# One expert in three items of 256 rows with lists known step by step, the other seven in items of 768 rows

## The chip, the cores and the metric

The kernel runs on one core of a Trainium2 chip. The core has five engines that run their own instructions in order: TensorE (PE; its weight loads are PEld), VectorE (DVE), ScalarE (ACT), GpSimd (POOL) and SyncE (SP); SyncE issues most DMAs, GpSimd those that gather and scatter rows by an index. The metric is the device time of one execution in microseconds, the median of several runs. A profile is one execution with its own time; its rows are shown further down.

## What is computed

A gated linear attention over 4 sequences of 768 steps and 8 heads of 48, whose output is the input of a mixture of 8 experts with 2 chosen for each of the 3072 tokens (32-bit floats throughout):

```python
f = 1.0 / (1.0 + np.exp(-f_logit))
for t in range(S):
    state = f[:, :, t, :, None] * state + np.einsum('bhd,bhe->bhde', k[:, :, t], v[:, :, t])
    y[:, :, t] = np.einsum('bhd,bhde->bhe', q[:, :, t], state)
x = y.transpose(0, 2, 1, 3).reshape(B * S, H * D)           # 3072 x 384
noisy = x @ w_gate + np.log1p(np.exp(x @ w_noise)) * noise  # 8 experts
# top2: the two largest of each token; top2_w: softmax of the two
for e in range(E):
    for k in range(2):
        mask = top2[:, k] == e
        h = np.maximum(x[mask] @ w1[e], 0.0)                # 384 -> 1024
        out[mask] += top2_w[mask, k, None] * (h @ w2[e])    # 1024 -> 384
```

## The kernel before

**Attention.** The sequence is cut into 6 chunks of 128 steps, and with 4 sequences that makes 24 rounds. A round has seven stages: `forget` (transposes f, exponential and logarithm on ScalarE), `summed` (a running sum on VectorE), `decays` (exponentials on ScalarE), `scaled` (transposes q and k, products on VectorE), `scores`, `output` and `features` (three blocks of matmuls). The loop over `i` (L1551) starts the stages of several rounds, each with its own lag, in an order written out by hand, and every engine's instructions stay in the order in which the loop issues them (`in_order`). Loads go into rings of 5 (f), 4 (q, k) and 6 (v) tiles by SyncE; `clamp` limits the f tile from below, on VectorE for the first two tiles, on GpSimd for the others. The first loads stand ahead of the loop. `warm_up` issues matmuls of ones while TensorE has nothing else, four in each of the three rounds before round 0. `load_router` brings the router's weights by eight small DMAs of GpSimd's queue.

**Router.** After a chunk's four rounds `route` finds the two experts of its 512 tokens and each token's place in its expert's list. Eight puts a chunk (`put`, L705, indirect DMAs of GpSimd) write the entries (row, gate, token) into `lists` in DRAM; the rows themselves lie in `x_rows`. A list grows chunk by chunk in order, so its first entries are final before the last chunk is routed. `first_loads` fetches and gathers the first lists within the attention's loop; what the kernel takes for granted about list lengths it checks with flags (`enough`, `plan`), and a raised flag starts the general path (`general`) behind the main one.

**Items.** The experts' work is cut into items, each a list of pairs (expert, first entry) of 256 rows; `p` counts pairs and `k` items. Three kinds exist before: items 0 and 1 are the first 256 rows of experts 0 and 1, taken from the lists of three chunks (`NE` = 2); items 2 and 3 are the other 512 rows of experts 1 and 0; items 4 to 9 are the 768 rows of experts 2 to 7 (`WIDE`). What a list has beyond 768 entries goes through five small remainder blocks (`quarter_block`), spread over five of the 768-row items.

- A 256-row item: `first_layer` (L955), four pieces of six matmuls `hp` and an activation by ScalarE, then `second_layer` (L1223), seven products of four matmuls (a Strassen form), each a piece. The product order is 1, 7, 4, 5, 6, 2, 3; their operands come from `second_sums` over w2 (VectorE, into `u`) and `inner_sums` over the hidden rows. The results of products are copied and scaled on ScalarE (`P17`, then the gates) and added on VectorE into `ys`, and two scatters (`scatter`, indirect DMAs that add) put them into `out`: one behind the fifth product, one behind the seventh.
- A 512-row item: `first_of_two` (L972), 44 matmuls of 256 columns with sums of weights and rows by VectorE (`first_sums`).
- A 768-row item: `first_of_three` (L1088), 15 products for each of four blocks of w1, in an order written out by hand (`ORDER`); sums of weights (`SUMS_W`) and of rows (`SUMS_T`) by VectorE are made during the item before. `late_second_layer` then runs three times, once for each 256 rows.

**Rows on their way to an item.** `fetch` reads 256 list entries (SyncE), `gather` brings their rows in two halves of 128 (GpSimd) into `xg`, a ring of four pairs. Rows must then be transposed. `turned` does it on TensorE (three transposes a half) with a copy out of PSUM. For 768-row items ScalarE parts the rows' 16-bit halves (`split`), SyncE issues a transposing DMA (`flip`), and ScalarE puts the halves together (`joined`). These steps stand between the products of the item before (`between`, in `second_parts`). A matmul over 256 columns needs both halves.

**Order around the change.** Behind the attention's loop the pieces of the items are issued one by one (L1643). Around each piece the loop issues zeros for `out` (SyncE, 192 KB each), fetches up to six pairs ahead, gathers by a rule on the item and the piece, one or two steps of the router, and all puts that are ready. Scatters of different items wait for each other, since they add to the same `out`. `weights` and `part_of_weights` load w1 and w2 into two places each, `home` says which item uses which; w2 of expert 1 is loaded in four parts between the attention and the loop over the items.

## Time and profile before

| | us |
|---|---|
| median of 3 runs | 623.33 |
| lowest and highest | 622.68, 626.96 |
| the profiled execution's own time | 622.47 |
| its span, first to last instruction | 620.7 |
| matmuls busy on TensorE | 605.5 |
| weight loads busy on TensorE | 555.6 |
| VectorE busy | 455.6 |
| ScalarE busy | 363.8 |
| GpSimd busy | 277.7 |

The span is that of the trace; the execution's time also has what lies around it. Busy times of engines overlap. The mean granted clock of TensorE over the span is 0.993 of full speed. Line numbers (L961) are those of the kernel before. A releaser is the last of what an instruction waited for, as far as the profile's semaphore events show it.

### The profile page before, as it was taken

The page shows a single profiled execution, that of the slowest core. Times are in us where ns is not written, and L with a number is a line of the kernel's source. Part 1 is how long each engine was busy: PE and PEld are TensorE (multiplying, and loading weights), DVE is VectorE, ACT ScalarE, POOL GpSimd, SP SyncE. Part 2 cuts the span into 40 slices and gives each one's busy share as a digit, 9 for nine tenths or more (in the row PEclk, how much of TensorE's full clock was granted, in tenths as well). Part 3 has the DMA queues.
Part 4 walks back from the last instruction along what each step waited for, and adds up shares of the span by engine and source line. Part 5 has one row for each costly group of instructions (what it writes and reads, how often), then busy time and mean ns, then how long its engine had stood idle before and what let it go on. Part 6 is the DMA issues. An engine that isn't in the chain of part 4 may idle for free.

```text
span 620.7 us, 13321 instructions
## 1 busy us (share of the span) xinstructions
PE 605.5 (98%) x4846; PEld 555.6 (90%) x4846; DVE 455.6 (73%) x1051; ACT 363.8 (59%) x890; POOL 277.7 (45%) x305
## 2 busy tenths in 40 slices
PE   8999999998999999999999999999999999999995
PEld 7999998887898889998899899899988998998995
DVE  6777868697575575888787887787877877877840
ACT  6877676753223343477756766676577467646611
POOL 6824688768774614052163316323440624241032
PEclk9999999999999999999999999999999999999998
DMA  9999988886907547368398559848873894361024
GB/s 182 191 231 200 194 170 171 187 182 195 282 8 231 128 134 168 129 108 256 128 216 179 154 154 204 242 105 218 136 254 118 204 209 129 71 145 23 0 26 56
DMA packets 183082, 98.00 MB, mean 158 GB/s; under 512 B 147600, under 2 KB 176272, under 8 KB 183008
## 3 DMA queue, kind: packets, MB, share of 16 engines
q1 hardware_dynamic: 170832, 77.81, 48.6%
q0 software_dynamic: 12176, 19.25, 17.3%
q8 instruction: 40, 0.66, 0.4%
q14 instruction: 34, 0.28, 0.2%
HBM read 69.68 MB, written 19.62 MB: 144 GB/s over the span
## 4 chain that ended last, share of the span: by engine, by line
PE 89%; DMA 4%; POOL 2%; DVE 1%; issue 1%; SPq 1%; ACT 0%; POOLq 0%; DVEq 0%; ACTq 0%
PE y L1293 30%; PE E L1123 7%; PE D L1123 7%; PE C L1123 5%; PE B L1123 5%; PE xp L628 4%; PE sc L575 4%; PE y L593 4%; PE hp L961 2%; PE y L604 2%; PE P L986 2%; PE kp L535 2%; PE A L1123 2%; PE fp L535 2%; PE ds L599 1%; PE qp L535 1%
## 5 line engine op out<-in xcount | busy, mean ns | idle before, releaser
L1170 POOL DMA_INDIRECT out_dram<-ys,slots x48 | 88.0, 1833 | 225.8 <-DVE ys L1299 156.4
L1293 PE MATMUL y<-qk_all,f_all 128*128 128x192 f32 x528 | 93.5, 326 | 1.0 <-ACT ys L1309 1.0
L1293 PEld LDWEIGHTS y<-qk_all,f_all 128*128 128x128 f32 x528 | 86.8, 190 | 1.6 <-ACT ys L1309 1.5
L1299 DVE SCALAR_TENSOR_TENSOR ys<-y,slots,ys 128x192 f32<-128x192 f32 x66 | 27.4, 416 | 55.6 <-PE y L1293 17.6
L855 POOL DMA_INDIRECT xg<-x_rows,slots x48 | 50.7, 1056 | 35.9 <-issue 23.5
L1293 PE MATMUL y<-w,hs_b 128*128 128x192 f32 x352 | 64.4, 326 | 0.0
L1293 PEld LDWEIGHTS y<-w,hs_b 128*128 128x128 f32 x352 | 58.6, 190 | 0.4
L707 POOL DMA_INDIRECT lists<-entry,sloti x48 | 51.2, 1066 | 10.5 <-issue 7.6
L1131 ACT ACTIVATE hs_b<-hs_b 128x256 f32<-128x256 f32 x120 | 50.2, 418 | 5.8 <-DVE hs_b L1135 4.4
L1342 ACT ACTIVATE ys<-y,slots 128x192 f32<-128x192 f32 x22 | 9.2, 420 | 58.5 <-PE y L1293 52.1
L608 ACT COPY yT<-y 128x256 f32<-128x256 f32 x48 | 15.7, 376 | 36.3 <-PE y L604 24.3
L578 DVE TENSOR_TENSOR A<-sc,causal 128x1024 f32<-128x1024 f32 x24 | 29.3, 1222 | 8.8 <-PE sc L575 8.6
L1293 PE MATMUL y<-qk_all,hs_b 128*128 128x192 f32 x176 | 32.9, 330 | 0.0
L1293 PE MATMUL y<-w,f_all 128*128 128x192 f32 x176 | 32.7, 329 | 0.0
L1293 PEld LDWEIGHTS y<-qk_all,hs_b 128*128 128x128 f32 x176 | 28.8, 190 | 2.4 <-issue 2.1
L900 ACT COPY planes<-xg 128x768 uint16<-128x768 uint16 x36 | 29.3, 826 | 2.5 <-DMA xg<-x_rows,slots 2.5
L549 DVE TENSOR_TENSOR_SCAN L<-f,cap 128x512 f32<-128x512 f32 x24 | 29.6, 1232 | 0.5 <-ACT cap L544 0.5
L1158 DVE TENSOR_TENSOR f_all<-hs_b 128x512 f32<-128x512 f32 x44 | 29.9, 683 | 0.0
L1293 PEld LDWEIGHTS y<-w,f_all 128*128 128x128 f32 x176 | 28.9, 190 | 0.7
L1009 ACT ACTIVATE hs_b<-hs_b 128x256 f32<-128x256 f32 x32 | 12.9, 417 | 27.0 <-DVE hs_b L1006 20.3
L1128 ACT COPY hs_a<-D 128x256 f32<-128x256 f32 x66 | 24.4, 370 | 7.2 <-PE D L1123 5.4
L529 POOL TENSOR_SCALAR f_all<-f_all 128x384 f32<-128x384 f32 x22 | 26.2, 1193 | 4.1 <-DMA f_all<-in_f_logit_dram 4.1
(282 smaller groups left out, 1583.7 us busy)
## 6 DMA issues: line engine op xcount, KB each, us to landing
w<-in_moe_w_dram SPq DMA_DIRECT2D x12, 1536.0 KB
w_q<-in_moe_w_dram SPq DMA_DIRECT2D x10, 1536.0 KB
w<-in_moe_w_dram SPq DMA_DIRECT2D x16, 384.0 KB
f_all<-in_f_logit_dram SPq DMA_DIRECT2D x24, 192.0 KB
...
```

The source lines that it names most:

```text
L535: nc.tensor.transpose(p[:, cols(hp)], flat[:, cols(hp)], ident)
L549: nc.vector.tensor_tensor_scan(L[n], data0=logf[n], data1=cap[n % 2].rearrange("d a t -> d (a t)"), initial=0.0, op0=ALU.add, op1=ALU.min)
L578: nc.vector.tensor_tensor(A[n].rearrange("j r (a i) -> j (r a) i", i=C), sc.rearrange("j r (a i) -> j (r a) i", i=C), causal.unsqueeze(1). ...
L707: into = nc.gpsimd.indirect_dma_start(out=lists, out_offset=bass.IndirectOffsetOnAxis(ap=sloti[:, r, b:b + 1], axis=0), in_=entry[:, c, b, ...
L855: nc.gpsimd.indirect_dma_start(out=xg[p][:, s, :], out_offset=None, in_=x_rows[0:HALF * B * C] if p < NE else x_rows, in_offset=bass.Indir ...
L900: nc.scalar.copy(planes[p][:, s], by_halves(p)[:, s * 2 * DM:(s + 1) * 2 * DM].rearrange("t (d h) -> t h d", h=2))
L1123: nc.tensor.matmul(banks[name, j], lhsT=half_of(x, k)[:, j * 128:(j + 1) * 128], rhs=half_of(y, k), start=first, stop=True, skip_group_che ...
L1131: nc.scalar.activation(at(to, j), at(y, j), AF.Relu, scale=-1.0 if more[0][0] == "-" else 1.0)
L1158: nc.vector.tensor_tensor(sm[which], x, y, op)
L1170: into = nc.gpsimd.indirect_dma_start(out=out, out_offset=bass.IndirectOffsetOnAxis(ap=slots[p][:, s, 2:3], axis=0), in_=ys[s], in_offset= ...
L1293: nc.tensor.matmul(to, lhsT=x[:, o, :], rhs=y[:, o, :], start=(start and o == 0), stop=(o == FH - 1), skip_group_check=not start)
L1299: nc.vector.scalar_tensor_tensor(to, in0=bank, scalar=gate[s], in1=to, op0=ALU.mult, op1=ALU.add)
```

## The change

`NE` becomes 3, and the items are: 0, 1 and 2 with rows 0 to 255, 256 to 511 and 512 to 767 of expert 0, then items 3 to 9 with 768 rows of experts 1 to 7. Items of 512 rows no longer exist, with `first_of_two`, `first_sums` and their helpers. Item 0 takes its rows from the lists of three chunks, as before; item 1 from those of five chunks; item 2 from the full lists (`known`). Item 1's list is fetched behind the 40th put, the last of chunk 4, and gathered behind the 42nd; in the attention's loop only item 0's list is left. A second check, `nearly_enough`, asks for 512 entries after five chunks. The groups that tell the scheduler which DMAs touch different rows (puts, zeros, scatters) follow.

Items 0 to 2 share the first places of w1 and w2, and the `u` sums of item 0 serve all three. Item 1's rows are turned between item 0's last two products, item 2's in item 1's second layer. The sums for item 3, the first of 768 rows, are made in items 1 and 2: `SUMS_W` in both, `SUMS_T` in item 2. Item 3's first pair is turned on TensorE in item 2's first layer, the other two are split and flipped there (behind its second and third step) and joined in its second layer. w2 of expert 1 is loaded in item 2's first four pieces. Remainder blocks start with item 4, as before.

At the start the first loads are in another order: the fourth and fifth f tile stand behind the second q and k tile, the first v tile in the loop. VectorE clamps the third f tile, the router's weights are loaded ahead of the loop, round 0 issues its `scores` ahead of `scaled` and `forget`, and the last of the three groups of four warm-up matmuls goes.

The diff, cut to its core (removed bodies of `first_of_two` and `first_sums` left out):

```diff
-    NE = 2
-    WIDE = 6
-    late_experts = (*range(NE - 1, NE - 3, -1), *range(NE, NE + WIDE), *range(NE - 3, -1, -1))
-    items = [(e, [(e, 0)]) for e in range(NE)]
-    items += [(e, [(e, 256 * i) for i in range(0 if e >= NE else 1, 3)]) for e in late_experts]
+    NE = 3
+    items = [(0, [(0, 256 * i)]) for i in range(NE)] + [(e, [(e, 256 * i) for i in range(3)]) for e in range(1, E)]
     pairs = [p for _, ps in items for p in ps]
     first_of = [sum(len(ps) for _, ps in items[:k]) for k in range(len(items) + 1)]
-    assert NE + WIDE == E and len(pairs) == NP
+    assert len(pairs) == NP
...
+            if c == NCH - 1:
+                tc.declare_no_dep(into.ins, group="nearly full", reason="slots differ")
...
-        lack = rt.tile([1, NE], F32, tag="lack", name="lack", bufs=1)
-        nc.vector.tensor_scalar(lack, total[0:1, 0:NE], 255.5, None, ALU.is_lt)
-        nc.vector.tensor_reduce(short, lack, axis=AX.X, op=ALU.max)
+        nc.vector.tensor_scalar(short, total[0:1, 0:1], 255.5, None, ALU.is_lt)
+        yield
+
+    def nearly_enough():
+        total = one_bank("total_c")[:, 0:E]
+        nc.tensor.matmul(total, lhsT=ones, rhs=upto[NCH - 2][:, :, B], start=True, stop=True)
+        yield
+        nc.vector.scalar_tensor_tensor(short, in0=total[0:1, 0:1], scalar=511.5, in1=short, op0=ALU.is_lt, op1=ALU.max)
         yield
...
     def home(k):
-        return k % NR if k < NE else (NE - 1 + k - NE) % NR
+        return 0 if k < NE else (k - NE + 1) % NR
+
+    def known(p):
+        return (HALF, NCH - 1, NCH)[min(p, 2)]
...
-        if p < NE:
+        if p == 0:
 
             tc.declare_no_dep(got.ins, group="later", reason="slots differ")
             tc.add_to_no_dep_group("full", got.ins)
+        elif p == 1:
+            tc.add_to_no_dep_group("nearly full", got.ins)
 
...
-            nc.gpsimd.indirect_dma_start(out=xg[p][:, s, :], out_offset=None, in_=x_rows[0:HALF * B * C] if p < NE else x_rows,
+            nc.gpsimd.indirect_dma_start(out=xg[p][:, s, :], out_offset=None, in_=x_rows[0:known(p) * B * C],
                                          in_offset=bass.IndirectOffsetOnAxis(ap=slots[p][:, s, 0:1], axis=0))
-            if p < NE:
+            if p == 0:
                 nc.gpsimd.memset(empty[:, 0:LR // 256], 0)
...
-        if NE <= k < NE + NR:
+        if k <= NE:
             return
...
+    def rows_of(k):
+        return wide[0] if k == 2 else xt_a[:, :, k * 256:(k + 1) * 256]
+
...
         k = item_of(p)
         if k < NE:
-            to = xt_a[:, :, k % 2 * 256 + s * 128:k % 2 * 256 + (s + 1) * 128]
+            to = rows_of(k)[:, :, s * 128:(s + 1) * 128]
...
-        (nc.vector.tensor_copy if p < NE else nc.scalar.copy)(to, xp[:, 0:DM].rearrange("d (k t) -> d k t", k=KO))
+        (nc.scalar.copy if p else nc.vector.tensor_copy)(to, xp[:, 0:DM].rearrange("d (k t) -> d k t", k=KO))
...
-            planes[p] = late[-1].tile([128, 2, 2, DM], U16, tag="planes", name=f"planes{p}", bufs=1)
+            if NE < p < NE + 3:
+                planes[p] = wide[1][:, p - NE].bitcast(U16).rearrange("t (s h d) -> t s h d", s=2, h=2)
+            else:
+                planes[p] = late[-1].tile([128, 2, 2, DM], U16, tag="planes", name=f"planes{p}", bufs=1)
...
-            most = min(NP if len(n_put) == NCH * B * 2 else NE, NP if what == "fetch" else done["fetch"])
+            most = min(NP if len(n_put) == NCH * B * 2 else 1, NP if what == "fetch" else done["fetch"])
...
-        if k == NE:
+        if 0 < k < NE:
             return
...
-    def first_sums(k, which):
...
-                    nc.tensor.matmul(hp[:, o, :], lhsT=w1[home(k)][:, i, (fo + o) * 128:(fo + o + 1) * 128], rhs=xt_a[:, i, k % 2 * 256:(k % 2 + 1) * 256],
+                    nc.tensor.matmul(hp[:, o, :], lhsT=w1[home(k)][:, i, (fo + o) * 128:(fo + o + 1) * 128], rhs=rows_of(k)[:, i, :],
...
+            if k:
+                sum_of_three(NE, SUMS_W[fo // 2 if k == 1 else 7 + fo // 2])
+            if k == 2:
+                if fo in (2, 4):
+                    turned(NE, fo // 4)
+                    split(NE + fo // 2, 0)
+                    split(NE + fo // 2, 1)
+                    flip(NE + fo // 2)
+                elif fo == 6:
+                    for t in SUMS_T:
+                        if t[0] == "0":
+                            sum_of_three(NE, t[2:])
             yield
...
-    def first_of_two(k):
...
-            if p < NE:
-                tc.declare_no_dep(into.ins, group="second half", reason="rows differ")
-                tc.add_to_no_dep_group("first half", into.ins)
+            if p < 2:
+                tc.declare_no_dep(into.ins, group=("second half", "last rows")[p], reason="rows differ")
+                tc.add_to_no_dep_group(("first half", "all but last")[p], into.ins)
...
+        if 0 < k + 1 < NE:
+            turns_now = {5: [(k + 1, 0)], 6: [(k + 1, 1)]} if k == 0 else {4: [(k + 1, 0)], 5: [(k + 1, 1)]}
+            if k == 1:
+                sums_now = {i + 1: [SUMS_W[4 + i]] for i in range(3)}
+        elif k + 1 == NE:
+            turns_now = {1: [(NE + 1, 0)], 2: [(NE + 1, 1)], 3: [(NE + 2, 0)], 4: [(NE + 2, 1)]}
+            split_now = {5: NE + 3}
+            sums_now = {3: [t[2:] for t in SUMS_T if t[0] == "1"], 4: [t[2:] for t in SUMS_T if t[0] == "2"]}
...
+        elif is_wide(k + 1):
+            turns_now = {2 + s: [(first_of[k + 1] + q, s)] for s in range(2)}
...
+            if not last:
+                split_now[1] = first_of[k + 1] + q + 1
+            elif is_wide(k + 2):
+                split_now[1] = first_of[k + 2]
...
-    for nm, n in (("f", 0), ("f", 1), ("q", 0), ("k", 0), ("f", 2), ("f", 3), ("q", 1), ("k", 1), ("v", 0)):
+    for nm, n in (("f", 0), ("f", 1), ("q", 0), ("k", 0), ("f", 2), ("q", 1), ("k", 1), ("f", 3), ("f", 4)):
...
-    clamp(2)
-    clamp(3)
...
+    for part in range(2):
+        load_router(part)
+    clamp(3)
...
-            m = (*(m for m in range(NS) if m % NCH < HALF), *(m for m in range(NS) if m % NCH >= HALF))[len(zeroed)]
+            m = [m for cs in (range(HALF), range(HALF, NCH - 1), (NCH - 1,)) for m in range(NS) if m % NCH in cs][len(zeroed)]
...
-        for what, p, pause in (("fetch", 1, 4), ("first", 0, 0), ("second", 0, 3), ("fetch", 2, 5), ("first", 1, 1), ("second", 1, 6),
-                               ("turned", 0, 0), ("fetch", 3, 1)):
+        for what, p, pause in (("fetch", 1, 4), ("first", 0, 0), ("second", 0, 15), ("turned", 0, 0)):
...
+        if i == 0:
+            order[0:3] = order[2], order[1], order[0]
...
-                load("f", n + 4)
+                for m in () if n < 2 else (n + 3,) if n < 5 else (n + 3, n + 4) if n == 5 else (n + 4,):
+                    load("f", m)
...
-                if n in (1, 2):
-                    load_router(n - 1)
+                if n < 2:
+                    load("v", n)
...
-                for m in (n + 1,) if n < 4 else (2 * n - 3, 2 * n - 2) if n < 6 else (n + 3,):
+                for m in () if n == 0 else (n + 1,) if n < 4 else (2 * n - 3, 2 * n - 2) if n < 6 else (n + 3,):
...
+            elif stage is summed and n == 0:
+                clamp(2, nc.vector)
...
-        if i < 0:
+        if i < -1:
...
-                router = chain(router, plan(), beyond())
+                router = chain(router, nearly_enough(), plan(), beyond())
...
-    for part in range(4):
-        part_of_weights(1, 2, part)
...
-        if item < NE or not is_wide(item + 2):
-            return 0
-        return 2 if item == NE else 1 if piece >= 12 else 0
...
+        if item == 2 and piece < 4:
+            part_of_weights(1, 2, piece)
...
-        n = item - NE - 2
+        n = item - NE - 1
...
+            if len(n_put) == (NCH - 1) * B * 2:
+                fetch(1)
+                done["fetch"] = 2
+            elif len(n_put) == (NCH - 1) * B * 2 + 2:
+                gather(1)
+                done["gather"] = 2
```

## Rows read from the trace of the kernel before

**Rows 1.** The page's busy time, share of the span and instructions of each engine.

```profile
PE 605.5 (98%) x4846; PEld 555.6 (90%) x4846; DVE 455.6 (73%) x1051; ACT 363.8 (59%) x890; POOL 277.7 (45%) x305
```

**Rows 2.** TensorE's stretches: the view by windows. Columns: from and to in us, length, busy us and instructions of TensorE's matmuls (PE), its weight loads (PEld), VectorE (DVE), ScalarE (ACT) and GpSimd (POOL), granted TensorE clock as a share of 2.4 GHz, busy share of the DMA engines, GB/s.

```profile
150.00:154.30 4.30, 2.40 (x31) 2.02 (x31) 1.75 (x7) 1.32 (x4) 3.97 (x6) 1.00 0.86 231
154.30:158.70 4.40, 4.39 (x13) 3.54 (x14) 0.95 (x2) 0.48 (x1) 3.91 (x6) 0.61 1.05 385
...
177.80:200.00 22.20, 21.39 (x120) 19.35 (x120) 12.98 (x32) 6.18 (x13) 12.37 (x14) 1.00 0.57 162
200.00:239.70 39.70, 38.73 (x213) 36.05 (x213) 24.98 (x57) 15.18 (x35) 15.99 (x13) 1.00 0.50 112
...
560.00:613.30 53.30, 53.20 (x288) 49.79 (x287) 32.46 (x71) 25.50 (x73) 10.99 (x7) 1.00 0.16 20
613.30:620.70 7.40, 0.00 (x0) 0.00 (x0) 0.00 (x0) 0.36 (x1) 1.55 (x1) 0.63 0.46 62
```

**Rows 3.** Who TensorE waited for: instruction and its line, what released it, us in total, times, longest.

```profile
PE hp L961 <- DVE xt_a L890: 1.9, 1, 1.9
...
PE y L1293 <- ACT ys L1309: 1.0, 1, 1.0
...
PE xgp L889 <- DMA xg<-x_rows,slots: 0.8, 1, 0.8
PE kp L535 <- DMA qk_all<-in_k_dram: 0.5, 1, 0.5
```

**Rows 4.** TensorE's instructions in order of time, those of one line merged: start, length, line, output and inputs, count (each matmul of two 32-bit operands is recorded twice, a transpose once). `hp` and `y` are a 256-row item's two layers, `xgp` the transposes of gathered rows, `E` the first product of a 768-row item.

```profile
167.35 1.46 PE L1237 MATMUL y<-w,hs_a 128*128 128x192 f32 x8
...
173.55 0.49 PE L889 MATMUL xgp<-ident,xg 128*128 128x128 f32 x3
173.88 1.47 PE L1237 MATMUL y<-qk_all,f_all 128*128 128x192 f32 x8
...
176.48 1.46 PE L1237 MATMUL y<-w,f_all 128*128 128x192 f32 x8
177.78 10.52 PE L961 MATMUL hp<-xt_a,w 128*128 128x256 f32 x48
...
277.16 0.59 PE L1123 MATMUL E<-xt_b,w 128*128 128x256 f32 x2
...
303.10 1.46 PE L1293 MATMUL y<-w,hs_b 128*128 128x192 f32 x8
```

**Rows 5.** The chain that ended last, in order of time: start, length, what it waited for. The first two are the third forget load and the third key load; the last three the landing of the last put, the fetch of the full lists and the landing of their first gather.

```profile
3.62 3.45 DMA f_all<-in_f_logit_dram
...
11.41 3.57 DMA qk_all<-in_k_dram
...
181.61 2.89 DMA lists<-entry,sloti
...
184.52 0.37 SPq L844
...
187.39 5.90 DMA xg<-x_rows,slots
```

**Rows 6.** ScalarE's instructions in order of time, with the idle time before them and its releaser.

```profile
15.53 0.63 ACT L554 ACTIVATE P<-L 128x512 f32<-128x512 f32 x1 [1.55 <-DVE L L549]
...
272.48 1.96 ACT L1373 COPY xt_b<-xg 128x768 uint16<-128x768 uint16 x2
...
325.34 0.83 ACT L900 COPY planes<-xg 128x768 uint16<-128x768 uint16 x1 [0.45 <-DMA xg<-x_rows,slots]
```

**Rows 7.** GpSimd's instructions in order of time. L707 is a put into the lists, L855 a gather, L1170 a scatter of an item's output, L1415 that of a small remainder block; from 160 to 206 us, and from 320 and 440 us.

```profile
166.76 1.04 POOL L707 DMA_INDIRECT lists<-entry,sloti  x1 [0.17 <-issue]
...
172.01 0.96 POOL L707 DMA_INDIRECT lists<-entry,sloti  x1 [0.17 <-issue]
...
192.72 1.65 POOL L1170 DMA_INDIRECT out_dram<-ys,slots  x1 [0.30 <-issue]
194.67 1.59 POOL L1170 DMA_INDIRECT out_dram<-ys,slots  x1 [0.30 <-issue]
202.08 1.55 POOL L1170 DMA_INDIRECT out_dram<-ys,slots  x1 [5.82 <-DMA out_dram<-ys,slots]
...
205.79 1.01 POOL L855 DMA_INDIRECT xg<-x_rows,slots  x1 [0.30 <-DMA out_dram<-ys,slots]
...
321.60 1.01 POOL L855 DMA_INDIRECT xg<-x_rows,slots  x1 [1.75 <-DMA slots<-lists]
...
445.58 1.56 POOL L1170 DMA_INDIRECT out_dram<-ys,slots  x1 [4.00 <-DVE qk_all L1086]
451.06 1.34 POOL L1415 DMA_INDIRECT out_dram<-ys_q,slots_q  x1 [3.91 <-DMA out_dram<-ys,slots]
```

**Rows 8.** ScalarE's groups by line: count, busy us and mean ns, idle time before them. L900 is `split`, L1373 `joined`, L963 the activation of a 256-row item's first layer.

```profile
L900 ACT COPY planes<-xg 128x768 uint16<-128x768 uint16 x36 | 29.3, 826 | 2.5 <-DMA xg<-x_rows,slots 2.5
L1373 ACT COPY xt_a<-xg 128x768 uint16<-128x768 uint16 x24 | 25.2, 1054 | 0.0
...
L963 ACT ACTIVATE hs_a<-hp 128x512 f32<-128x512 f32 x8 | 4.8, 597 | 16.9 <-PE hp L961 16.9
```

**Rows 9.** SyncE's queue in order of time: the issue of one `flip`.

```profile
266.78 1.45 SPq L903 DMA_TRANSPOSE xg<-planes  x1
```

**Rows 10.** VectorE's groups by line: one of the `second_sums`.

```profile
L933 DVE TENSOR_TENSOR qk_all<-w 128x768 f32<-128x768 f32 x18 | 17.0, 950 | 0.0
```

143 lines of the change are left out of this document (14 added, 129 removed).

## The prediction

> **What bounds the kernel now.** I read the page's busy times first: TensorE has work for 605.5 of 620.7 us, VectorE for 73% and ScalarE for 59% [rows 1]. So time is won only where TensorE's instructions are removed or where it waits, and lost only where a new wait ends on it. The second view is TensorE by stretches: of the last 768-row item's 53.30 us 53.20 are busy, the closing 7.4 us hold no matmul and stay as they are [rows 2]. The third is what TensorE waited for: 1.9, 1.0, 0.8 and 0.5 us are the waits that matter here [rows 3]. The wait of 1.9 us falls into 150 to 154.3, where TensorE was busy 2.40 of 4.30 us; behind it the granted clock is 0.61 for 4.4 us, that is mostly the lower of the two levels (1.2 and 2.4 GHz) [rows 2]. Those 4.4 us hold one piece of six matmuls, 2.6 us at the price below: 1.8 us lost to the clock. This stretch is not touched by the change (item 0 is fetched, gathered and turned at the same steps of the loop), so I leave it in. The profiled run lasted 622.47 us for a span of 620.7, 1.8 us outside; the median of the three runs is 623.33, 0.9 above the profiled run.
>
> **What is removed on TensorE.** 44 matmuls of a 512-row item are two such items' 88, and 24 a 256-row item's. Before: 2 x 24 + 2 x 44 + 6 x 60 = 496; after: 3 x 24 + 7 x 60 = 492. Sixty take 303.10 - 277.16 = 25.9 us, 0.432 each [rows 4]: 1.7 us less. Transposes of gathered rows: before six lists of 256 x 2 halves x 3 = 36, after four lists = 24; three take 173.88 - 173.55 = 0.33 us [rows 4], so 12 less are 1.3 us. The second layer is 28 matmuls for each 256 rows in either kernel.
>
> By stretches it comes to more, since waits go too. From the start of item 1's first layer (177.78) to the first product of the first 768-row item (277.16) are 99.4 us [rows 4]. After the change the same start leads, one 768-row item further, over: two 256-row items of 24 x 0.432 + 7 x 1.30 (177.78 - 176.48) + 2 x 0.33 = 20.2, with 0.1 of the small count 20.3, and one 768-row item of 25.9 + 21 x 1.30 = 53.2. That is 93.8, 5.6 less, and 5.4 with the added total of five chunks (0.14 as the other such total). In it are the 3.0 of instructions, the 0.8 us wait of the transposes for rows of the full lists and the 1.0 us at the end of the first 512-row item [rows 3]; the other 0.8 is slower starts behind them. **Gain 5.4 if nothing new waits.**
>
> **Start-up.** The third key load was the 13th of SyncE's queue and landed at 14.98 (11.41 + 3.57), the third forget load, the 5th, at 7.07 [rows 5]: 1.0 us a load. TensorE waited 0.5 us for that key load [rows 3]. It is now 11th, 2.0 earlier. Scores of round 0 no longer stand behind two other stages, and four warm-up matmuls go. But at 15.53 ScalarE had waited for VectorE's third scan [rows 6], and VectorE now gets the masking of the first scores ahead of the two products before that scan: what the later start of the mask saved there is spent, and that chain moves by little, 0 to 0.5. On GpSimd's queue the eight router loads now stand ahead of the clamp of the fourth forget load, which TensorE wants a stage later than before. Bounds: 1.5 gained (TensorE's own order) and 0.5 lost (a wait in the thinned warm-up). I take 0.7, nearer the chain.
>
> **Item 1 now needs five chunks' lists.** The last put of chunk 4 starts at 166.76; a put lands 2.9 after its start (181.61 to 184.50), and the first gather starts 2.9 after the fetch (184.52 to 187.39) [rows 5, 7]: 172.5. On GpSimd the gather stands behind the second put of chunk 5 (172.01, 1.6 each) and so starts at 173.6. A gather that started at 321.60 let ScalarE go on at 325.34 [rows 6, 7]: 3.7 us. So the first half is there at 177.3. TensorE comes to its transposes at 167.35 + six products + the small matmuls = 175.8 [rows 4]: it waits 1.5. Then 0.33, a product, 0.33, and the copy to SBUF has no cover before the first layer: 0.8. Item 1 starts 2.3 later than it could.
>
> **Item 2 and the full lists.** The two gathers stand ahead of six puts on GpSimd. Six puts of 1.6 from 176.1 put the last at 184.0 (before: 181.61), and the full lists are fetched 2.4 us later, first gather 189.8 (before: 187.39) [rows 5, 7]. GpSimd now issues six gathers (before: four) ahead of item 0's two scatters: 1.33 each (187.39 to 192.72 for four) to 197.8; second scatter 199.7. Item 1's scatters wait for it to land: 7.4 us from start to next start with zeros on the DMA engines (194.67 to 202.08), 5.5 without (445.58 to 451.06) [rows 7]. They start at 205.2 to 207.1 and take 3.7 (202.08 to 205.79), so the gather of the list of rows 512 to 767 of expert 1 starts at 208.9 to 210.8. I take 209.8.
>
> That gather decides, since item 2's third step of the first layer puts two ScalarE copies of 0.83 (`split`) on those rows, ahead of the activation of its fourth step. Halves land at 213.6 and 214.9, copies end 215.7, activation 0.60 [rows 8]: 216.3. TensorE wants that activation for the third product of the second layer. Without waits it is there at 177.9 + 20.3 + 11.1 (first layer of item 2 with two transposes) + 2 x 1.30 = 212.0, so it is 4.3 late; item 1's 2.3 is inside this, not added to it. Queued behind the blocked copies on ScalarE are the copies of P17, the gate products and four `joined` copies; SyncE's transpose of these rows and two parts of w2 of expert 1 wait too, which VectorE wants only at the end of the first piece of item 3.
>
> **Start of item 3.** Its first product needs both `joined` copies of that list. The last stands on ScalarE behind the scaling of the output, which follows the fifth product: from that product's end three VectorE steps, 0.6 + 0.4 of ScalarE and 1.05 [rows 8] make 3.2, and two products cover 2.6. The transpose itself took at most 5.7 (266.78 on SyncE to the copy at 272.48) [rows 6, 9], which can add 0.6. Behind come two more `split` copies, 1.7, before ScalarE frees the bank that the fourth product wants: 0.7 more. Bounds: 0.6 to 3; I take 1.9.
>
> **Sum.** 620.7 - 5.4 - 0.7 + 4.3 + 1.9 = 620.8. The same 0.1 on the median: **623.4 us, no change.** Costed at nothing: w2 of expert 1 in item 2 instead of before it (its cover is item 2's own 20 us), and the sums for the first 768-row item. They are 24 on VectorE in items 1 and 2; the second sums, four an item of 0.95 [rows 10], drop out there, since all three items share expert 0's weights. The flag that falls back to the general path isn't raised: from the reference's inputs I count 369 tokens of expert 0 in three chunks and 634 in five, with 256 and 512 needed.
>
> **Rivals.** (1) *The chain on GpSimd is hidden.* If gathers and scatters land sooner, ScalarE is never blocked and only 2.3 + 1.3 remain: 620.7 - 5.4 - 0.7 + 3.6 = 618.2, 620.8 on the median. For it speaks that gathers kept `split` waiting only 2.5 us in all [rows 8]; against it, that two scatters are in series ahead of this one. It needs the gather 3 us earlier.
> The Trainium skill ("DMA: Bandwidth & Descriptors", Anatomy of one DMA) gives about 2.0 us plus bytes over 436 GB/s for a DMA from GpSimd, an estimate of 2.5 us for these 196 KB. By it gather and scatter together land 4 us sooner, and this rival holds; the rows, 3.7 and 5.5 from the start of the issue, speak for the forecast.
> (2) *Everything is hidden*, item 1's lists too: 620.7 - 5.4 - 1.5 = 613.8, 616.4. Against it: the copy before item 1 has no cover.
> (3) *The clock falls at the new waits: slower.* Behind the 1.9 us wait the clock cost 1.8 us; behind those of 1.0 and 0.8 us it stayed at 1.00 [rows 2]. TensorE's wait in item 2 is 2.0 once item 1's is taken off, and that before item 3 1.3 to 2.5. If both go over about 1.9, 2 x 1.8 come on top: 627.0. A fall at item 1's wait costs nothing, since the chain on GpSimd ends later anyway.
> (4) *It does not do what it says:* the gather of item 1 ends up behind all eight puts. Then item 1 waits 9.6 more less what the chain takes back, some 5: 628. By the order of the loop the 42nd put releases it, so this is unlikely.
>
> **Chances.** Forecast 0.52, with its own range 621 to 626; rival 1 0.25, between 617.1 and 621; rival 2 0.07; rival 3 0.13; rival 4 0.03. A change of 1%, 6.2 us, is about what a measurement of this kernel can tell from none. Faster by over 1% is rival 2 (0.07); slower by over 1% needs rivals 3 or 4 at their upper ends (0.05); the rest, 0.88, is within 1%. The range for 8 in 10 takes the forecast, rival 1 and rival 3: 617.5 to 628.
>
> **What would show it.** Right: TensorE has 492 such matmuls and 24 transposes of gathered rows; `xgp` waits some 1.5 us for `xg` near 176 and `hp` 0.8 for ScalarE; the first full-list gather starts about 2.4 us later; ScalarE waits 3 us or more for `xg` in `planes`, and TensorE right behind it for `hs_a`; the last 768-row items are 53.3 us as before. Wrong: no ScalarE wait at `planes` in item 2 (rival 1), a granted clock under 0.8 there (rival 3), or start-up more than 1.5 us off. The forecast fails altogether if the items of 768 rows show waits that they did not have.

## The result, and the profile after

The changed kernel takes 628.06 us (median of 21 executions, 624.12 to 630.81) against 623.5 (622.17 to 627.41) for the kernel before: a ratio of 1.0067, with a 95% interval of 1.0048 to 1.0085. That is slower by two thirds of a per cent, inside the 1% that was given most of the chance. The forecast was 623.4 us, with a range of 617.5 to 628: applied to the 623.33 us from which the forecast started, the ratio gives 627.5, just inside. It lies outside 621 to 626, the forecast's own range, and next to the 627.0 of rival 3. The profiled execution took 627.73 us, its span is 625.7 (before 620.7), its mean clock 0.992.

Who TensorE waited for, after (in us: total, times, longest); it answers to [rows 3]:

```profile
PE y L1130 <- ACT hs_a L947: 3.9, 1, 3.9
PE xgp L890 <- DMA xg<-x_rows,slots: 1.7, 1, 1.7
...
PE hp L945 <- ACT xt_a L891: 0.6, 1, 0.6
PE E L1020 <- ACT xt_b L1266: 0.4, 1, 0.4
```

The waits foreseen are all there: 1.7 for item 1's rows and 0.6 for their copy, and the large one in item 2's second layer (y). TensorE in order of time, answering to [rows 4]: first item 0's start in the kernel before, then the changed kernel.

```profile
154.31 4.54 PE L961 MATMUL hp<-xt_a,w 128*128 128x256 f32 x12 [1.91 <-DVE xt_a L890]
```

```profile
154.10 2.86 PE L945 MATMUL hp<-xt_a,w 128*128 128x256 f32 x12 [0.27 <-DVE xt_a L891]
...
175.99 0.52 PE L890 MATMUL xgp<-ident,xg 128*128 128x128 f32 x3 [1.67 <-DMA xg<-x_rows,slots]
...
178.70 10.63 PE L945 MATMUL hp<-xt_a,w 128*128 128x256 f32 x48 [0.57 <-ACT xt_a L891]
...
210.26 1.46 PE L1130 MATMUL y<-w,hs_a 128*128 128x192 f32 x8
217.53 1.65 PE L1130 MATMUL y<-qk_all,hs_a 128*128 128x192 f32 x4 [3.85 <-ACT hs_a L947]
...
224.98 1.46 PE L1130 MATMUL y<-w,f_all 128*128 128x192 f32 x8
226.88 0.70 PE L1020 MATMUL E<-xt_b,w 128*128 128x256 f32 x2 [0.44 <-ACT xt_b L1266]
```

Item 0 starts at 154.10 (before 154.31), and its first twelve matmul records take 2.86 us (before 4.54, at 0.61 of the clock [rows 2]). Item 1 starts at 178.70, item 3 at 226.88, item 4 (the second item of 768 rows) at 280.99; the first item of 768 rows of the kernel before started at 277.16. Behind the wait of 3.85 us the rest of the second layer, 217.53 to 226.44, takes 8.9 us. The view by windows (from:to, length, busy us and instructions of TensorE, granted clock, DMA share, GB/s; compare [rows 2]) says why:

```profile
206.00:217.50 11.50, 7.68 (x42) 0.95 0.78 171
217.50:219.00 1.50, 1.47 (x5) 0.50 0.56 111
219.00:221.50 2.50, 2.50 (x9) 0.50 1.00 219
221.50:223.70 2.20, 2.20 (x10) 0.60 1.03 385
223.70:226.80 3.10, 2.74 (x17) 1.00 0.95 379
```

For 6 us the clock is mostly at the lower of its two levels (1.2 of 2.4 GHz), behind the wait. What TensorE waited for stands in ScalarE's rows: it sat 6.91 us in front of `split` (L904) of expert 1's rows 512 to 767, with the activation (L947) that TensorE wanted queued behind it.

```profile
215.42 1.56 ACT L904 COPY hs_b<-xg 128x768 uint16<-128x768 uint16 x2 [6.91 <-DMA xg<-x_rows,slots]
216.89 0.59 ACT L947 ACTIVATE hs_a<-hp 128x512 f32<-128x512 f32 x1
...
220.70 1.05 ACT L1266 COPY xt_b<-xg 128x768 uint16<-128x768 uint16 x1 [0.52 <-DMA xg<-hs_b]
224.93 0.62 ACT L1158 ACTIVATE ys<-ys,slots 128x384 f32<-128x384 f32 x1 [3.19 <-DVE ys L1157]
...
225.80 1.03 ACT L1266 COPY xt_b<-xg 128x768 uint16<-128x768 uint16 x1
```

And on GpSimd the gather of those rows (p=5) stands behind item 1's scatters, which by the program wait for item 0's to land (compare [rows 7]). Item 0's second scatter started at 199.24, item 1's first 6.2 us later; the releaser that its row names only ended last there (in e5 it is another, a copy into xt_a).

```profile
188.40 0.98 POOL L853 DMA_INDIRECT xg<-x_rows,slots  x1 [3.69 <-issue]
...
205.47 1.91 POOL L1067 DMA_INDIRECT out_dram<-ys,slots  x1 [4.64 <-ACT hs_a L947]
207.69 1.56 POOL L1067 DMA_INDIRECT out_dram<-ys,slots  x1 [0.31 <-issue]
209.55 1.01 POOL L853 DMA_INDIRECT xg<-x_rows,slots  x1 [0.30 <-issue]
```

It starts at 209.55 (forecast 209.8), but ScalarE gets its first half only at 215.42, 5.9 us later; the forecast had 3.7. The activation behind it ends at 217.48, forecast 216.3.

### The profile page after: what moved, and what is told of

Same layout as the page of the kernel before. It is cut to its first block, busy times and chain, and to the rows that moved or that the text cites. A ratio compares the mean times of both kernels' runs of the same rounds, so it can differ in the third digit from the quotient of the medians.

```text
span 625.7 us, 13297 instructions
## 1 busy us (share of the span) xinstructions
PE 605.4 (97%) x4820; PEld 554.2 (89%) x4820; DVE 451.0 (72%) x1045; ACT 377.4 (60%) x920; POOL 277.0 (44%) x302
## 4 chain that ended last, share of the span: by engine, by line
PE 61%; issue 2%; DMA 2%; DVE 1%; POOL 1%; ACT 1%; POOLq 0%; DVEq 0%; ACTq 0%
PE y L1186 29%; PE D L1020 8%; PE E L1020 8%; PE C L1020 6%; PE B L1020 6%; PE A L1020 2%; PE yp_q L1302 1%; PE hp_q L1285 1%; DMA out_dram<-ys,slots 1%; DMA xg<-x_rows,slots 1%; POOL out_dram L1067 1%; PE y L1130 1%; DVE qk_all L983 0%; DVE f_all L1055 0%; ACT hs_b L904 0%
## 5 line engine op out<-in xcount | busy, mean ns | idle before, releaser
L1067 POOL DMA_INDIRECT out_dram<-ys,slots x48 | 89.9, 1873 | 229.5 <-DVE ys L1192 145.2
L1186 PE MATMUL y<-qk_all,f_all 128*128 128x192 f32 x504 | 88.9, 326 | 0.0
L1186 PEld LDWEIGHTS y<-qk_all,f_all 128*128 128x128 f32 x504 | 83.0, 190 | 0.3 <-ACT ys L1211 0.3
L1028 ACT ACTIVATE hs_b<-hs_b 128x256 f32<-128x256 f32 x140 | 58.5, 418 | 6.9 <-DVE hs_b L1032 4.4
L1186 PE MATMUL y<-w,hs_b 128*128 128x192 f32 x336 | 61.5, 326 | 0.0
L1186 PEld LDWEIGHTS y<-w,hs_b 128*128 128x128 f32 x336 | 55.9, 190 | 0.4
L704 POOL DMA_INDIRECT lists<-entry,sloti x48 | 49.8, 1037 | 12.6 <-issue 7.8
L1025 ACT COPY hs_a<-D 128x256 f32<-128x256 f32 x77 | 28.5, 370 | 8.4 <-PE D L1020 5.0
L1186 PE MATMUL y<-qk_all,hs_b 128*128 128x192 f32 x168 | 31.4, 330 | 0.1
L904 ACT COPY planes<-xg 128x768 uint16<-128x768 uint16 x36 | 29.6, 824 | 2.4 <-DMA xg<-x_rows,slots 1.3
L1025 ACT COPY hs_a<-E 128x256 f32<-128x256 f32 x63 | 23.4, 372 | 10.9 <-PE E L1020 8.5
```

What stands on the lines that cost most here:

```text
L704: into = nc.gpsimd.indirect_dma_start(out=lists, out_offset=bass.IndirectOffsetOnAxis(ap=sloti[:, r, b:b + 1], axis=0), in_=entry[:, c, b, ...
L904: nc.scalar.copy(planes[p][:, s], by_halves(p)[:, s * 2 * DM:(s + 1) * 2 * DM].rearrange("t (d h) -> t h d", h=2))
L1025: nc.scalar.copy(at(to, j), banks[more[0], j])
L1028: nc.scalar.activation(at(to, j), at(y, j), AF.Relu, scale=-1.0 if more[0][0] == "-" else 1.0)
L1067: into = nc.gpsimd.indirect_dma_start(out=out, out_offset=bass.IndirectOffsetOnAxis(ap=slots[p][:, s, 2:3], axis=0), in_=ys[s], in_offset= ...
L1186: nc.tensor.matmul(to, lhsT=x[:, o, :], rhs=y[:, o, :], start=(start and o == 0), stop=(o == FH - 1), skip_group_check=not start)
```

## The experiments

Chips differ: the kernel before took 616.7 to 617.6 us on the chips of e1 to e10, 622.0 on that of e11 and e12, and 623.5 beside the changed kernel (the slower sort below). Each ratio is therefore to the kernel before on the run's own chip; across chips only traces are compared, and each trace is one execution.

| run | ratio to before (95%) | median, lowest, highest | before there | mean clock of the executions |
|---|---|---|---|---|
| changed kernel | 1.0067 (1.0048 to 1.0085) | 628.06, 624.12, 630.81 | 623.5 | 0.990 to 0.997 |
| e1 | 1.0066 (1.0046 to 1.0086) | 621.61, 616.81, 626.22 | 616.81 | 0.989 to 0.997 |
| e2 | 1.007 (1.0056 to 1.0083) | 621.19, 620.85, 621.61 | 616.81 | 0.996 to 0.998 |
| e3 | 1.0114 (1.0097 to 1.0131) | 624.32, 623.57, 625.24 | 616.81 | 0.987 to 0.993 |
| e4 | 1.0007 (0.999 to 1.0025) | 616.74, 615.01, 620.61 | 616.81 | 0.995 to 0.999 |
| e5 (changed kernel again) | 1.0112 (1.0076 to 1.0148) | 623.37, 621.56, 629.65 | 617.55 | 0.987 to 0.995 |
| e6 | 1.0083 (1.006 to 1.0107) | 622.48, 620.42, 624.77 | 617.55 | 0.988 to 0.996 |
| e7 | 1.0089 (1.0061 to 1.0116) | 621.88, 617.1, 626.0 | 617.55 | 0.989 to 0.997 |
| e8 | 1.01 (1.0059 to 1.0142) | 622.59, 621.52, 630.15 | 617.55 | 0.964 to 0.995 |
| e9 | 1.007 (1.005 to 1.009) | 621.67, 619.54, 622.62 | 616.71 | 0.990 to 0.997 |
| e10 | 1.0006 (0.999 to 1.0022) | 617.43, 615.04, 619.84 | 616.71 | 0.993 to 0.998 |
| e11 | 0.9934 (0.991 to 0.9958) | 619.12, 617.77, 621.11 | 622.03 | 0.996 to 0.998 |
| e12 | 0.9965 (0.9942 to 0.9989) | 620.12, 617.85, 623.58 | 622.03 | 0.994 to 0.998 |

e1 to e4 share a chip, so do e5 to e8, e9 and e10, and e11 and e12.

**e1: the gather ahead of item 1's scatters.**

```diff
-            ahead("gather", NE + 2 if item < NE - 1 else ...
+            ahead("gather", NE + 2 + item if item < NE - 1 else ...
```

> The gather of expert 1's rows 512 to 767 (p=5) is issued with item 1, ahead of item 1's two scatters, instead of with item 2 behind them; nothing else. Theory A (the loss is the ScalarE copies of split(5) behind that gather, and the granted clock that falls at TensorE's wait there): the gather starts near 201 us instead of 209.6, the copies have their rows, TensorE's wait of 3.85 us for hs_a in item 2 goes, the clock stays at 1.00 there, item 3 starts 5 to 6.5 us earlier: some 622 us, ratio to before 0.995 to 0.999. Rival B (item 1's wait for five chunks' lists, or the start of item 3 itself, takes the time; the gather only shows it): item 3 starts less than 2 us earlier, ratio 1.004 or more.

The gather started at 196.83, `split` found its rows, and TensorE's wait in item 2 was gone. The time was not: the ratio is 1.0066. The next link was late instead. The rows of ScalarE, of SyncE and of TensorE in order of time, of e1:

```profile
219.26 1.04 ACT L1266 COPY xt_b<-xg 128x768 uint16<-128x768 uint16 x1 [7.63 <-DMA xg<-hs_b]
```
```profile
206.22 2.56 SPq L907 DMA_TRANSPOSE xg<-hs_b  x1
208.83 1.26 SPq L873 DMA_DIRECT2D w<-in_moe_w_dram  x1
210.20 0.66 SPq L863 DMA_DIRECT2D w<-in_moe_w_dram  x1
```
```profile
222.12 1.22 PE L1020 MATMUL E<-xt_b,w 128*128 128x256 f32 x2 [6.90 <-ACT xt_b L1266]
```

The transposing DMA issued at 206.22 gave ScalarE its rows at 219.26, 13 us later; in the changed kernel it took 3.7 (217.01 to 220.70), with the DMA engines at 0.56 in its first microseconds (the window from 217.50 above). This profiled execution is the longest of the run (626.22) and has another wait of 3.1 us, at 330.78, so the rows show the kind of the wait, not its usual size; the shortest execution took 616.81. e7 and e10, which keep this edit, have a shorter wait at the same place and none in item 2. So theory A was right on the first link and wrong that it was the only one, and rival B's ratio came true for a reason that neither named.

**e2: TensorE kept busy in the wait.**

```diff
+        if k == NE - 1:
+            busy = one_bank("busy")
+            for _ in range(16):
+                nc.tensor.matmul(busy[:, 0:128], lhsT=ones, rhs=ones, start=True, stop=True)
         product(4, a(1, 1), u[4])
```

> Sixteen matmuls of 128 columns into a bank that nobody reads stand ahead of the third product of item 2's second layer, so that TensorE works where it waited for ScalarE; the wait itself is not shortened. Theory A (half of the loss is the clock behind the wait): granted clock 1.00 instead of 0.50 to 0.60 at 217.5 to 223.7, the five products after the wait take 6.5 us instead of 9, 2 to 3 us less than the changed kernel: ratio to before 1.002 to 1.004. Rival (the clock behind that wait costs nothing, since item 3 waits for ScalarE's joined copies anyway, or falls all the same): ratio as for the changed kernel, 1.005 to 1.0085.

The clock stayed up, and the rest of the second layer took 6.2 us (213.52 to 219.71). The view by windows of e2, columns as above:

```profile
213.50:216.00 2.50, 2.48 (x15) 1.00 0.79 151
216.00:219.70 3.70, 3.70 (x23) 1.00 0.98 314
```

The ratio, 1.007, is the rival's. It equals the changed kernel's first 1.0067; e5, the changed kernel on another chip, has 1.0112, and its interval overlaps that of e2. So the times do not tell what the fall of the clock behind this wait costs. By the traces it is 1.4 to 2.0 us: from the product behind the wait to item 3's first it takes 7.4 us in e2 (213.52 to 220.90), 8.8 in e5 and 9.35 in the changed kernel. 4.4 us of loss remain with the clock at full speed, and 4.1 by the traces (item 0's first product to item 4's: 124.5 here, 120.5 in e4 on the same chip): the fall is a part of the loss, not all. e2's five executions lie 0.8 us apart and e5's six 8 us, but the kernel before, without this wait, spreads over 2.6 to 5.3, so what the fall does to the scatter is not shown.

**e3: `split` and `flip` of p=5 behind the activation of the fourth step on ScalarE.**

```diff
-                    split(NE + fo // 2, 0)
-                    split(NE + fo // 2, 1)
-                    flip(NE + fo // 2)
+                    if fo == 2:
+                        split(NE + 1, 0)
+                        split(NE + 1, 1)
+                        flip(NE + 1)
                 elif fo == 6:
+                    split(NE + 2, 0)
+                    split(NE + 2, 1)
+                    flip(NE + 2)
```

> Only the order on ScalarE: in item 2 the two copies of split(5) and the transpose behind them are emitted after the activation of the first layer's fourth step instead of ahead of it; the gather stays where it is, near 209.6 us. Theory A1 (the late gather reaches TensorE only through the activation queued behind the copies): TensorE's wait for hs_a falls under 1 us, the second layer runs on, item 3 then waits for its joined copies at 222 to 224 us instead of 226.9: 2 to 4 us less than the changed kernel, ratio 1.000 to 1.003. Rival (the wait only moves to the start of item 3, clock included): item 3 starts at 226 or later, ratio 1.005 or more.

The wait in item 2 went, and one of 7.4 us at the start of item 3 took its place; the rival held. Part of it is the edit's own doing: `flip` now also stands behind the load of w1 for item 4 (1.5 MB) on SyncE's queue, and the lower clock followed this wait too. SyncE in order of time, and who TensorE waited for, of e3:

```profile
206.75 0.44 SPq L863 DMA_DIRECT2D w<-in_moe_w_dram  x1
214.89 1.44 SPq L907 DMA_TRANSPOSE xg<-hs_b  x1
```
```profile
PE E L1024 <- ACT xt_b L1270: 7.4, 1, 7.4
```

**e4: the start-up part alone**, put into the kernel before.

```diff
-    for nm, n in (("f", 0), ("f", 1), ("q", 0), ("k", 0), ("f", 2), ("f", 3), ("q", 1), ("k", 1), ("v", 0)):
+    for nm, n in (("f", 0), ("f", 1), ("q", 0), ("k", 0), ("f", 2), ("q", 1), ("k", 1), ("f", 3), ("f", 4)):
...
+        if i == 0:
+            order[0:3] = order[2], order[1], order[0]
```

> The kernel before with the start-up part of the change alone (order of the first loads, of the clamps and the router loads, scores first in round 0, no warm-up after the third round); items as before. Prediction's term: 0.7 us gained, bounds -0.5 to 1.5: ratio 0.9975 to 1.001. Theory S0 (the lead is eaten by small waits before item 0): 0 to 0.3 us, ratio 0.9995 to 1.001. Rival S2 (the start-up part also takes away the 1.9 us wait and the clock fall behind it at the start of item 0, which the profile of the changed kernel does not show): granted clock 1.00 at 154 to 159 us, 2 us gained, ratio 0.996 to 0.998.

1.0007: no gain that can be measured on this chip, as theory S0 has it. In its profile item 0's first twelve matmul records took 2.86 us, at full clock, as rival S2 has it; in the profile of the kernel before they took 4.54. That profile is from the slower sort of chip, and none of the kernel before was taken on this one, so whether the start-up removes the fall is open.

**e5: the changed kernel again.**

> The changed kernel itself, unedited, as the common measure for the other runs of this call. Both theories: ratio to before 1.005 to 1.0085; a wait of 3 us or more for hs_a in item 2, and behind it some us at the lower clock.

1.0112, somewhat above the expected interval; its trace has the same wait of 3.75 us in item 2, and 0.50 and 0.66 of the clock in the 4 us behind it.

**e6: w2 of expert 1 back ahead of the loop.**

```diff
-        if item == 2 and piece < 4:
-            part_of_weights(1, 2, piece)
...
     zeros(4)
+    for part in range(4):
+        part_of_weights(1, 2, part)
     for _ in first_pairs:
```

> One part of the change undone: the four parts of w2 of expert 1 are loaded ahead of the loop over the items, as before, instead of at the first four steps of item 2. The gather stays behind the scatters. Theory D (DMA work of 1.5 MB in item 2 makes the gather and the transpose of that list late): the gather of p=5 lands 1 to 2 us sooner (4 to 5 us after its start instead of 5.8), the wait for hs_a in item 2 falls to 2 to 3 us; 1 to 3 us less than the changed kernel, ratio 1.002 to 1.005. Rival (the move costs nothing, as the prediction had it; the place of the gather on GpSimd's queue alone decides): within 1 us of the changed kernel, ratio 1.005 to 1.0085.

The first half of the gather landed 4.0 us after its start (205.84 to 209.87), and TensorE's wait in item 2 was 1.0. But the load delayed the puts of chunk 4, and so item 1's list, and now the clock fell there. Nor was the activation in item 2 sooner: the second half, issued at 207.25 next to the transpose of p=4 (207.24), landed only at 213.37, 6.1 us later and with no weights beside it, and ScalarE needs both halves. The activation starts 63.3 us after item 0's first product, in e5 62.0; the wait is short because TensorE itself came later. Who TensorE waited for, the view by windows, and ScalarE's two `split` copies, of e6:

```profile
PE xgp L890 <- DMA xg<-x_rows,slots: 2.0, 1, 2.0
...
PE y L1130 <- ACT hs_a L947: 1.0, 1, 1.0
```
```profile
172.90:176.50 3.60, 2.90 (x14) 0.70 0.14 42
176.50:179.00 2.50, 2.43 (x6) 0.50 0.01 1
```
```profile
209.87 0.83 ACT L904 COPY hs_b<-xg 128x768 uint16<-128x768 uint16 x1 [1.24 <-DMA xg<-x_rows,slots]
213.37 0.83 ACT L904 COPY hs_b<-xg 128x768 uint16<-128x768 uint16 x1 [2.67 <-DMA xg<-x_rows,slots]
```

So neither place was free, and the ratio is the rival's. The time is 0.9 us less than e5's by the medians, and the intervals overlap.

**e7: gather early, w2 ahead of the loop, w1 of item 4 behind item 2's second layer.** The edits of e1 and e6, and:

```diff
-            if fo == FO - 2:
+            if fo == FO - 2 and k < NE - 1:
                 ahead(1, k + NR + 1)
...
         product(3, sm[4], b(1, 1))
+        ahead(1, k + NR + 1)
         ahead(2, k + NR + 1)
```

> Three edits: the gather of p=5 goes with item 1 (as in the run with that edit alone), w2 of expert 1 is loaded ahead of the loop, and the load of w1 for the second 768-row item (1.5 MB) goes from the end of item 2's first layer to the end of its second layer, behind the transpose of p=5. Theory D (with the gather early the next thing late is the transpose of p=5, because 2.6 MB of weights share the DMA engines with it): the transpose lands 4 to 6 us after its start instead of 13, TensorE's wait of 6.9 us for xt_b at the start of item 3 falls under 2 us; ratio 0.997 to 1.001. Rival G (it is the gathers of the next item's rows and the scatters, all on GpSimd's queue, that share the engines with the transpose, not the weights): the wait stays at 4 us or more, ratio 1.004 or more.

In the profiled execution the wait at the start of item 3 fell to 1.4 us and item 4 started 122.5 us after item 0 (126.0 in e5): 617.10 us, as theory D has it. But that is the fastest of six; the others took 621 to 626 at mean clocks of 0.989 to 0.994, and the ratio, 1.0089, is past the rival's. What is left in the trace is the wait that the early w2 makes in item 1, 3.2 us; the puts (L704) took twice as long to land as in e5. The issues of 156 to 174 us, in e5 and then in e7 (count, KB each, median us from issue to landing):

```profile
lists<-entry,sloti POOLq DMA_INDIRECT x9, 3.2
```
```profile
w<-in_moe_w_dram SPq DMA_DIRECT2D x4, 384.0 KB
...
lists<-entry,sloti POOLq DMA_INDIRECT x7, 6.4
```

**e8: the gather, split and transpose of p=6 later.** As e7, and:

```diff
-            split_now = {5: NE + 3}
...
-        return 1 if is_wide(item + 2) and (piece >= 12 or item == 2) else 0
+        return 1 if is_wide(item + 2) and (piece >= 12 or item == 2 and piece >= 8) else 0
...
         for n, text in enumerate(ORDER):
             steps(text)
+            if k == NE and n in (3, 4):
+                split(first_of[k + 1], n - 3)
+                if n == 4:
+                    flip(first_of[k + 1])
```

> As the run before in this call, and besides the gather of p=6 (first rows of the second 768-row item) goes behind the first scatter of item 2, and its split and transpose into item 3's first layer, behind the fifth row of its order. Theory D: little more is won, 0 to 1 us. Rival G: the wait for xt_b at the start of item 3 goes now (under 1.5 us), ratio 0.996 to 1.000. Whichever holds, item 3 then starts within 2 us of the last product of item 2.

1.01, past the rival's range; its interval is too wide to tell theory D's gain of 0 to 1 us. The profiled execution (630.15 us, mean clock 0.964) ran at 0.94 to 0.97 of the clock for its first 450 us and tells only the order: ScalarE no longer waited for the transpose, and the 1.0 us wait that stayed at item 3 is the second `joined` copy behind the scaling of the output. Item 1's wait was 3.4 us.

**e9: w2 in the gap behind item 1's gather.**

```diff
                 gather(1)
                 done["gather"] = 2
+                held = ffn.tile([128, 4], F32, tag="held", name="held", bufs=1)
+                nc.sync.dma_start(out=held, in_=xg[1][:, 1, 0:4])
+                for part in range(4):
+                    part_of_weights(1, 2, part)
```

> The changed kernel with one edit: the four parts of w2 of expert 1 stand on SyncE's queue behind a copy of 16 bytes a partition from item 1's gathered rows, so that they load when that gather has landed, at 171 to 176 us, where the DMA engines are idle (share 0.02 to 0.05 in the profiles of this kernel), and no longer in item 2. It differs from the run that loaded them before the loop in that nothing of item 1's lists waits for them. Theory D (w2's 1.5 MB in item 2 makes the gather of p=5 late): the gather lands 4 to 5 us after its start, TensorE's wait for hs_a in item 2 is 1.5 to 3 us instead of 3.75, TensorE's wait in item 1 stays at 1 to 1.7; 1 to 3 us less than the changed kernel. Rival (the place on GpSimd's queue alone): wait in item 2 of 3.3 us or more, within 1 us of the changed kernel. Both: the executions still scatter over several us, with lower mean clocks in the longer ones.

The gather landed in 3.9 us (207.34 on GpSimd, 211.27 on ScalarE), about as theory D has it. But it started 2 us later than in e5: the load, at 174 to 181, fell among the last puts, so the full lists came later (first gather 187.12, in e5 183.65). The wait in item 2 was still 3.4 us, as the rival has it, and the clock fell behind it. Without w2 beside it the gather's first half took 3.9 and 4.0 us (e9, e6; the DMA engines at 0.87 and 0.90), with it 5.2 to 6.4 (changed kernel, e5, e2, e3; at 1.10 to 1.17). That is six traces, and the second half in e6 shows that other transfers do it too.

**e10: everything that the runs point to.** e1's gather, e9's w2, e7's w1, and:

```diff
                 if fo in (2, 4):
                     turned(NE, fo // 4)
-                    split(NE + fo // 2, 0)
-                    split(NE + fo // 2, 1)
-                    flip(NE + fo // 2)
+                if fo in (0, 4):
+                    split(NE + 1 + fo // 4, 0)
+                    split(NE + 1 + fo // 4, 1)
+                    flip(NE + 1 + fo // 4)
...
-            turns_now = {1: [(NE + 1, 0)], 2: [(NE + 1, 1)], 3: [(NE + 2, 0)], 4: [(NE + 2, 1)]}
+            turns_now = {1: [(NE + 1, 0)], 2: [(NE + 1, 1)], 3: [(NE + 2, 0), (NE + 2, 1)]}
```

> All that the runs before point to in one kernel: the gather of p=5 with item 1; w2 of expert 1 in the idle gap behind item 1's gather; w1 of the second 768-row item behind item 2's second layer; the split and transpose of p=4 one step of the first layer earlier, so that the two transposes do not queue; both joined copies of p=5 ahead of the scaling of the output on ScalarE. If the causes found are all there is (late gather, crowded transpose, clock behind the waits): TensorE waits 1.0 and 0.6 us at item 1 and under 0.7 us from there to item 3; from the first product of item 0 to that of the second 768-row item 118 to 120 us (126 in the changed kernel's profile, 120.5 in the kernel before with the new start-up); executions within 3 us of each other; ratio to before 0.995 to 0.999. If something else is lost that the traces do not show: ratio above 1.001, or executions that scatter by 5 us and more.

1.0006: the loss is gone, a gain is not there yet. e9, on the same chip and with the same place for w2, has 1.007, so the other edits together are worth 4 us; they were not run apart there. From item 0's first product to item 4's it took 121.3 us (150.13 to 271.38). Two waits are left at item 3, 1.7 us for the transpose, which took 9 us (205.38 to 214.59), and 1.0 for ScalarE. SyncE and ScalarE in order of time, of e10:

```profile
205.38 2.60 SPq L907 DMA_TRANSPOSE xg<-hs_b  x1
```
```profile
214.59 1.95 ACT L1268 COPY xt_b<-xg 128x768 uint16<-128x768 uint16 x2 [3.28 <-DMA xg<-hs_b]
```

**e11 and e12: p=6 later as well, and TensorE busy in item 1's wait.** e11 is e10 with e8's edit; e12 is e11 and:

```diff
+        if k == 0:
+            busy = one_bank("busy")
+            for _ in range(4):
+                nc.tensor.matmul(busy[:, 0:128], lhsT=ones, rhs=ones, start=True, stop=True)
         between(5)
```

> As e10_all_ahead, and the gather of p=6 stands behind item 2's first scatter, its split and transpose in item 3's first layer behind the fourth and fifth rows of its order (the edit of e8_next_gather_later), so that nothing of GpSimd's queue but item 1's scatters shares the DMA engines with the transpose of p=5. Theory D (crowded transpose): both joined copies of p=5 run without waiting for the transpose, TensorE's waits of 1.7 and 1.0 us at the start of item 3 go, item 4 starts 2 to 3 us earlier than in e10_all_ahead (some 119 us after item 0's first product): ratio 0.995 to 0.998. Rival (the transpose of p=5 is slow by itself, 8 us, whoever shares the engines): wait of 1 us or more for xt_b stays, ratio 0.999 to 1.002.

> As the run before in this call, with four matmuls of 128 columns into an unread bank between item 0's sixth and seventh products of the second layer, where TensorE waits 1.0 us for item 1's rows. If the clock still falls behind that wait in some executions: the executions lie closer together (within 2 us) and the median is 0.5 to 1.5 us lower than in the run before. If a wait of 1.0 us costs nothing but itself: the same median within 0.6 us, the same scatter.

Both beat the kernel before on their chip, 0.9934 and 0.9965, and their intervals overlap. Neither expectation for the four matmuls came: the median is 1.0 us higher with them and the scatter wider (5.7 us for 3.3), so nothing shows that they help; in e11's trace the clock stayed at 1.00 behind the wait anyway. In e12 ScalarE did not wait for the transpose at all (at most 5.8 us, 209.22 to 215.03), and item 3 starts without a wait, as theory D has it; in e11 it took 8 us again (210.19 to 218.42, with a scatter issued at 210.10 beside it), as the rival has it. The two kernels differ only in those matmuls, so what makes the transpose slow is not settled. TensorE's first products of items 3 and 4 in e12, and ScalarE in e11:

```profile
218.59 0.59 PE L1021 MATMUL E<-xt_b,w 128*128 128x256 f32 x2
...
272.84 0.60 PE L1021 MATMUL E<-xt_b,w 128*128 128x256 f32 x2
```
```profile
218.42 1.96 ACT L1271 COPY xt_b<-xg 128x768 uint16<-128x768 uint16 x2 [2.28 <-DMA xg<-hs_b]
```

From item 0's first product to item 4's it is 120.8 us in e11 and 119.5 in e12; 121.3 in e10, 126.0 in e5, 126.9 in the changed kernel's profile, 120.5 in e4, 122.9 in the kernel before. By these traces e11 is only 0.5 us ahead of e10, so most of the step from 1.0006 to 0.9934 seems to belong to the chips. Against e4, which has the new start-up and the old items, e12 is only 1.0 us shorter: item 1 starts 2.8 us later behind item 0 (24.6 us for 21.8), and from there to item 4 it takes 3.8 less (94.9 for 98.7). On the slower sort the profile of the kernel before has the fall of the clock at item 0 (1.7 us), and no profile with the new start-up has it; whether that is the difference was not run (e4 on a chip of that sort would tell). So how much of e11's and e12's gain belongs to the items is not shown.

## Why the prediction was right, and which steps failed

It was right that the time would move by less than 1%, and right on which wait decides and where it stands. It was 4.7 us too low on the median, and 4.9 on the span (620.8 against 625.7). By its own signs rival 3 came as well (a granted clock under 0.8 in item 2), and it is rival 3 that had set the upper end of the range, at which the time came out. Its steps one by one:

- **What is removed**: right. Transposes of gathered rows are 24 for 36. In e12, where next to nothing waits, item 1's first product to item 4's takes 94.9 us (177.93 to 272.84), against 93.9 forecast without waits and 99.4 before: 4.5 of the 5.4 us are there when nothing waits.
- **Start-up, 0.7**: not found on the chip of e4 (1.0007), within its bounds; in the changed kernel's profile item 0 starts 0.2 us sooner. There item 0's clock did not fall, 1.7 us that the forecast had left in as not touched by the change. That was luck for the time of item 1.
- **Item 1, 1.5 + 0.8**: 1.67 and 0.57. Together with the clock of item 0 it starts at 178.70; the forecast comes to 179.4.
- **The full lists and the gather's place**: the gather of p=5 started at 209.55, forecast 209.8. The way there had two errors that nearly cancel: the first full-list gather started at 188.40 (forecast 189.8, 1.0 us later than before and not 2.4), and six gathers took 8.9 us up to item 0's scatter where 8.0 were forecast.
- **"Halves land at 213.6/214.9"**: the first step that failed. The 3.7 us came from one gather, at 321.60 in the kernel before, beside which the DMA engines were at 0.98 and moved 172 GB/s. Here they were at 1.13 and moved 258 GB/s (209.5 to 215.4), and it took 5.9. The wait was 3.85 where 2.0 (4.3 less item 1's 2.3) was forecast: the activation ended 1.2 us later than forecast, and TensorE came 0.6 sooner. The sentence that costs w2 of expert 1 at nothing goes with it: it asked when VectorE wants w2, not what the load slows on its way. Without w2 the first half takes 3.9 to 4.0 (e6, e9), but in neither run was the activation sooner (63.3 and 62.8 us after item 0's first product, in the changed kernel 62.8), so w2 is at most a part of it, and how large a part is not shown.
- **Rival 3 apart from the forecast**: the second. With a wait of 3.85 us the clock fell, and the rest of item 2 took 8.9 us instead of the 6.2 of e2: 2.7, of which the shorter wait at item 3 took 0.7 back. The mechanism was there, priced 1.8 a fall and given 0.13 for two falls; one came. But it was not another case: it hung on the forecast's own wait, which was already at its condition ("about 1.9").
- **Start of item 3, 1.9**: within its bounds, 0.44 us of wait and 0.9 in its first products (starts of E 1.69, 1.40 and 2.14 us apart, later 1.30, 1.29 and 1.73), with `joined` behind the scaling as described. In e2 and e5 the wait is 1.18.

The sum over the span, against the forecast: item 1's start -0.7; from there to item 4's start 102.3 for 97.8, of which the wait is 1.85, the clock 2.7, the start of item 3 -0.55 and 0.5 small gaps; 0.8 in the six last items and 0.4 behind the last matmul, both unexplained and of the size by which one kernel's profiles differ (item 4's to the last item's start: 283.5 here, 282.8 in e5).

Rival 1 (everything on GpSimd hidden, 618.2) would have been wrong even with its condition met. Run e1 had the gather 8.5 us sooner than e2 on the same chip, more than the 3 it asked for, and the time stayed; in its trace the transpose was next. The prediction bounded the transpose by 5.7 us, from one at 266.78 with the DMA engines at 0.87; it took 3.7 to 13. The Trainium skill ("DMA: Bandwidth & Descriptors", SWDGE vs HWDGE vs iDMA) says that a DMA engine takes turns between the queues that GpSimd and SyncE feed; the slow transposes of e1, e10 and e11, with GpSimd's transfers beside them, agree, but no run separates these from the weights, and e12's took at most 5.8 with a scatter issued 1.6 us before it. The estimate of 2.5 us that the prediction worked out from the Trainium skill ("DMA: Bandwidth & Descriptors", Anatomy of one DMA) was below every gather read here, 3.7 to 6.4 from the start of the issue.
